# Half of one chunk's first product moved to Strassen's form, with its activations, sums and loads rearranged

## The chip, the core and the metric

The kernel runs on one core of a Trainium2 chip. A core has TensorE (PE: matmuls; its weight loads are listed apart as PEld), VectorE (DVE), ScalarE (ACT), GpSimd (POOL) and SyncE (SP, which here only issues transfers). Each engine works through its own queue in order, and semaphores make one wait for another. Matmul results go to PSUM, which has eight banks of 512 fp32 columns; everything else is in SBUF. The metric is the device time of one execution in microseconds (us), lower is better. Times below are from the start of the profiled span.

## The reference

Two stages. The first is a linear attention: q is put through a softmax over the head dimension, k through one over the sequence; per batch and head a 64 x 64 matrix kv is formed, and q times kv is the output. The second is a feed-forward layer with Silu between two products.

```python
q_s = softmax(q, axis=-1); k_s = softmax(k, axis=2)     # 8 batches, 8 heads, 576 rows, 64 columns
kv  = einsum('bhsd,bhse->bhde', k_s, v)
x   = einsum('bhsd,bhde->bhse', q_s, kv)                 # laid out as 4608 x 512
h   = x @ w_in                                           # 512 x 2048
out = (h * sigmoid(h)) @ w_out                           # 2048 x 512
```

Inputs and output are fp32.

## The kernel before, in words

The 4608 rows are taken in nine chunks of 512 columns of the transposed x (`XT`); batches have 576 rows, so chunk 0 is handled together with the 64 columns that follow it, and chunk 1 has only 448 columns of its own (`pieces(1)`, columns 64 to 511). For each chunk the first product (`XT` by `W1`, 16 blocks of 128 output features) and Silu give `GT0` or `GT1` in turn, and the second product (`GT` by `W2`) gives the output.

A list `units` holds closures that issue TensorE's work one after the other; `plan(u, f)` says which other operations are issued just before unit `u`. The last loop walks through the list. So the order on every engine is written out by hand: each engine's queue holds its operations in the order in which this walk meets them, and a late operation holds everything behind it on its engine.

Stages:

- Opening (to about 15 us): batch 0's loads on SP, W1's and W2's parts and batch 1's and 2's loads on GpSimd's queue; attention of batch 0.
- Wide phase, 16 units from about 15 to 33 us: chunk 0's first product with 576 columns (`wide_mm`, L256), two banks each, three pairs in turn. `silu` does Tanh on ScalarE (L248, h times half the sum of one and tanh(h/2) is Silu) and one combining operation on VectorE (L249). Batch 1's exps stand on ScalarE between the tanhs: `exp_q` (L108) before units 9 and 11, `exp_k` (L111) before 13 and 15. The sums of `q` go by `qsum_pair` on GpSimd (L124, L127), `qsum_end` on VectorE and `qnorm` (L155), on GpSimd for the first half and on VectorE for the second.
- From `b1` on (33 us), 32 units: chunk 0's second product, 16 plain blocks `mm2_plain` (L396) into banks 2 to 5, and chunk 1's first product, 16 plain blocks `mm1` (L276) of four matmuls with 448 columns, into banks 0 to 3; the first ten second-product blocks go alone, then the two kinds in turn, then the ten remaining first-product blocks alone. Between them: transposes (`tr`, L173) and `kv` (L187) and `xt` (L226) of batch 1, then those of batch 2, whose q is transposed by a DMA on SP (`q_transpose`, L165).
- `full(t)`, t from 2 to 6, 28 units each of eight matmuls with 256 columns, and two more chunks in the same form without new loads. Here both products are in Strassen's form as Winograd wrote it: seven products in the place of eight, for the price of sums. The first product of chunk t (`group`, L359, two halves g of eight blocks each) alternates with the second of chunk t-1 (`prod`, L458). The sums need `WS` (of W1, `ws_op` L312), `XS` (of XT, `xs_op` L321), `T` (of W2, `t_op` L442) and `S` (of GT, `s_op` L432). `group` puts products 1, 6, 7 and 4 into banks 0 and 1, and 2, 5 and 3 into banks 2 and 3; `group_snap` copies the first pair out to `h` (ScalarE, or VectorE where said), `group_add` adds the second pair to it on VectorE (L337), and `group_silu` is a Silu on ScalarE (L343) from `h` or straight from PSUM.
- `end`: the last chunk's second product. Products 1, 2, 6, 5, 7, 4, 3 in turn; `part` combines and stores the pieces (L705, L720).

Before the change the W sums are made here: `WS` and the first two `T` on VectorE between `b1`+3 and `b1`+20, and T4 and T3 (in place of a part of W2) on GpSimd at `b1`+22. The loads of batch 3 are issued on SP before unit `b1`+20, those of batch 2 on GpSimd before 10 (q), `b1` (k) and `b1`+6 (v).

`ld` has two buffers for each of `qt`, `kt`, `vt`, so a load waits until the half of the batch before it has been read. One `h0`, `h1`, `h2` each exist. `eq` has one buffer.

Of the kernel before, what the change touches and what calls it, by code (L numbers as in the profile page):

```python
# [12 lines left out]
ALU = mybir.AluOpType  # L13
# [4 lines left out]
def kernel(  # L18
# [86 lines left out]
    def exp_q(b, cc):  # L105
        if "eq" not in st[b]:
            st[b]["eq"] = ap.tile([128, J, NG * D], BF16, name="eq")
        nc.scalar.activation(out=half(st[b]["eq"], cc), in_=jgd(b, "qt", cc), func=ACT.Exp)  # L108
# [162 lines left out]
    A1_BANKS = [0, 1, 0, 1, 0, 1, 2, 0, 3, 1, 0, 2, 1, 0, 2, 3]  # L271

# [11 lines left out]
    def mm1_silu(t, fb, bank):  # L284
        o0 = pieces(t)[0][3]
        silu(t, fb, PS[:, bank, o0:TCH], GTS[t % 2][:, fb, o0:TCH], TCH - o0)

    def mm1(t, i):
        mm1_mm(t, FB[i], A1_BANKS[i], range(NC))
        mm1_silu(t, FB[i], A1_BANKS[i])  # L290

# [5 lines left out]

    def wa(c, f):
        return W1[:, 2 * c:2 * c + 2, f * 128:(f + 4) * 128]

    def xb(t, c, n):
        return XTS[t % 2][:, 2 * c:2 * c + 2, (1 - n) * HT:(2 - n) * HT]
# [11 lines left out]
    def xs_op(t, i):  # L314
        in0, in1 = {
            1: (xb(t, 0, 1), xb(t, 0, 0)),
            2: (xb(t, 1, 1), XS4[0]),
            3: (xb(t, 1, 1), xb(t, 0, 1)),
            4: (xb(t, 1, 0), XS4[1]),
        }[i]  # L320
        nc.vector.tensor_tensor(out=XS4[i - 1], in0=in0, in1=in1, op=ALU.subtract)  # L321

    def group_out(t, f, n):
        return GTS[t % 2][:, f:f + 4, (1 - n) * HT:(2 - n) * HT]

    def four(x):
        return x.rearrange("p (f n) -> p f n", f=4)

    def group_bank(bank):
        return PS[:, bank:bank + 2, :].rearrange("p b (f n) -> p (b f) n", f=2)  # L330

    def group_snap(i, eng=nc.scalar):
        H[i] = mp.tile([128, 2 * TCH], FP32, name=f"h{i}", bufs=1)
        copy(eng, H[i], PS[:, 0:2, :].rearrange("p b n -> p (b n)"))

    def group_add(i):
        nc.vector.tensor_tensor(  # L337
            out=H[i], in0=PS[:, 2:4, :].rearrange("p b n -> p (b n)"), in1=H[i], op=ALU.add
        )

    def group_silu(t, i, f, n):
        x = group_bank(0) if i is None else four(H[i])
        nc.scalar.activation(out=group_out(t, f, n), in_=x, func=ACT.Silu, scale=1.0 / XS)  # L343

    def group(t, g, i, on=None, defer=False):
        bank = 0 if i in (1, 6, 7, 4) else 2
# [10 lines left out]
        for p in range(4):  # L357
            for c in range(2):
                nc.tensor.matmul(  # L359
                    out=PS[:, bank + p // 2, (p % 2) * HT:(p % 2 + 1) * HT],  # L360
                    lhsT=a[:, c, p * 128:(p + 1) * 128],
                    rhs=bb[:, c, :],
# [5 lines left out]
        if i == 1:  # L368
            group_snap(0)
        elif i == 2:  # L370
            group_add(0)
        elif i == 6:
            group_snap(1, on.get(1, nc.scalar))
        elif i == 7:
            group_snap(2, on.get(2, nc.scalar))
            group_add(2)
        elif i == 4:
            group_silu(t, None, f1, 0)
        elif i == 3:
# [3 lines left out]
            group_add(1)  # L383
# [245 lines left out]
    a1 = [lambda i=i: mm1(1, i) for i in range(NFB)]  # L629

    units += [lambda i=i: mm2_plain(0, i) for i in range(10)]
    for i in range(10, NFB):
        units += [a1[i - 10], lambda i=i: mm2_plain(0, i)]
    units += a1[NFB - 10:]
    four_pairs = "ggbgbgbgbbgbgb"


# [65 lines left out]
    def part(name, bank, th, n, a):  # L703
# [13 lines left out]
            (0, 1): (nc.scalar, nc.gpsimd) if a == 0 else (nc.sync, nc.sync),  # L717
# [7 lines left out]
    def end(i, m):  # L725
        if i in (5, 3):
            prod(last, i, m, bank=(4, 0)[m], fresh=(i == 5), done=(i == 3))
        elif i == 4:
            prod(last, i, m, bank=1, fresh=(m == 0), done=(m == 1))
        else:  # L730
            prod(last, i, m, bank=5 if i == 2 else 3)
        if i == 3:
            part("sb", (4, 0)[m], 0, 1, m)
        elif m == 1 and i in (1, 6, 7):
            snap(last, {1: "sa", 6: "sb", 7: "sc"}[i], 3)
# [6 lines left out]
        elif m == 1 and i == 4:  # L742
            part("sc", 1, 1, 0, 0)
            part("sc", 1, 1, 0, 1)
# [8 lines left out]
    def loads(b, eng):  # L753
        for name, src in (("qt", q), ("kt", k), ("vt", v)):
            for cc in range(2):
                load(b, name, src, cc, eng)

    plan(9, lambda: (load_w2(8, 12), exp_q(1, 0), qsum_pair(1, 0)))
    plan(10, lambda: (load(2, "qt", q, 0, nc.gpsimd), load(2, "qt", q, 1, nc.gpsimd)))
# [76 lines left out]
```

## Time and profile before

| | |
|---|---|
| median of 4 runs | 266.0 us (265.73 to 266.6) |
| the profiled execution | 266.6 us, span 264.8 us |
| TensorE busy | 254.4 us (96%), 2708 matmuls |
| VectorE busy | 210.5 us (79%) |
| ScalarE busy | 182.7 us (69%) |
| GpSimd busy | 75.7 us (29%) |
| granted TensorE clock | 0.999 of full speed |
| from 35 to 55 us: TensorE, VectorE, ScalarE, GpSimd busy | 19.3, 19.4, 11.1, 10.7 of 20 |
| from 55 to 75 us | 19.7, 17.4, 15.3, 12.9 of 20 |
| T4, T3 on GpSimd | 4.07 and 4.06 us, at 57.2 and 61.3 |

Matmuls overlap, so a busy TensorE is not one at its peak: the distance from start to start says more. In the rows of the timeline the columns are: start, duration (of all merged instructions together), engine, source line, operation, output and inputs with shapes, count, and in brackets the idle time before it with what released it. In the chain of work that ended last each piece is start, duration, and what worked or was waited for.

### The profile page before, as it was taken

How to read it: one execution, taken by the hardware profiler on the slowest of the kernel's cores; microseconds unless marked ns; L12 is line 12 of the kernel's file. 1: busy time of each engine (PE TensorE's matmuls, PEld its weight loads, DVE VectorE, ACT ScalarE, POOL GpSimd, SP SyncE). 2: the span in 40 equal slices, each digit the busy share in tenths (PEclk: the TensorE clock that was granted, in tenths of full speed). 3: DMA queues.
4: the chain of work that ended last, by engine and by line, in shares of the span. 5: the costliest groups of instructions: out<-in, count | busy, mean ns of one | idle time of the engine just before them, and what ended most of it. 6: DMA issues, size and time to landing. Idle time of an engine off the chain costs nothing.

```text
span 264.8 us, 6375 instructions
## 1 busy us (share of the span) xinstructions
PE 254.4 (96%) x2708; PEld 200.8 (76%) x2708; DVE 210.5 (79%) x276; ACT 182.7 (69%) x209; POOL 75.7 (29%) x65
## 2 busy tenths in 40 slices
PE   8799999999999999999999999999999999999993
PEld 3357644445888888878888888888888888888782
DVE  2966789987997999789979997999798448855832
ACT  5756964749796699659966996699664757584610
POOL 1743991498341305030513050305000000000004
PEclk9999999999999999999999999999999999999999
DMA  7999999569987488747964887450416003300634
GB/s 253 333 189 339 253 332 334 214 121 378 333 308 138 163 188 305 160 143 149 336 137 164 186 305 154 153 125 0 92 22 139 0 2 81 80 2 1 131 69 119
DMA packets 35452, 45.89 MB, mean 173 GB/s; under 512 B 16208, under 2 KB 19984, under 8 KB 35424
## 3 DMA queue, kind: packets, MB, share of 16 engines
q1 hardware_dynamic: 29568, 33.69, 45.8%
q0 software_dynamic: 5616, 11.60, 16.7%
q8 instruction: 21, 0.34, 0.5%
q10 hardware_dynamic: 240, 0.20, 0.3%
q14 instruction: 7, 0.06, 0.1%
HBM read 36.70 MB, written 9.44 MB: 174 GB/s over the span
## 4 chain that ended last, share of the span: by engine, by line
PE 63%; DVE 17%; DMA 9%; issue 4%; POOL 3%; ACT 2%; POOLq 0%; DVEq 0%; ACTq 0%
PE PS L458 30%; PE PS L359 26%; DMA qt<-in_q_dram 5%; DVE GT L249 3%; DVE h L337 3%; DMA qT<-eq 2%; DVE zq L146 2%; DVE S L432 2%; PE PS L276 2%; PE PS L226 2%; PE PS L187 1%; DMA W<-in_moe_w_in_dram 1%; DVE WS L312 1%; PE PS L396 1%; DVE zq L148 1%
## 5 line engine op out<-in xcount | busy, mean ns | idle before, releaser
L337 DVE TENSOR_TENSOR h<-PS,h 128x1024 f32<-128x1024 f32 x42 | 50.7, 1206 | 11.6 <-PE PS L359 6.2
L458 PEld LDWEIGHTS <-GT 128*128 128x128 f16 x512 | 49.6, 98 | 7.4 <-issue 1.6
L458 PE MATMUL PS<-W,GT 128*128 128x256 f16 x384 | 49.1, 273 | 0.4 <-DVE h L337 0.4
L359 PEld LDWEIGHTS <-WS 128*128 128x128 f16 x448 | 43.7, 98 | 5.7 <-issue 0.7
L155 POOL TENSOR_TENSOR eq<-eq,rzq 128x1152 bf16<-128x1152 bf16 x13 | 27.5, 2117 | 59.2 <-DVE rzq L150 59.2
L359 PE MATMUL PS<-XS,WS 128*128 128x256 f16 x336 | 43.5, 273 | 0.1
L343 ACT ACTIVATE GT<-h 128x1024 f16<-128x1024 f32 x42 | 43.3, 1054 | 0.3 <-DVE h L337 0.3
L89 ACT COPY h<-PS 128x1024 f32<-128x1024 f32 x32 | 32.4, 1012 | 13.7 <-PE PS L359 13.3
L458 PEld LDWEIGHTS <-S 128*128 128x128 f16 x384 | 37.2, 98 | 5.2 <-issue 1.0
L359 PEld LDWEIGHTS <-W 128*128 128x128 f16 x336 | 32.5, 98 | 4.4 <-issue 0.2
L458 PE MATMUL PS<-T,S 128*128 128x256 f16 x256 | 32.7, 273 | 0.0
L249 DVE SCALAR_TENSOR_TENSOR GT<-sg,PS 128x576 f16<-128x576 f32 (+1 forms) x32 | 21.2, 679 | 9.1 <-ACT sg L248 8.9
L359 PE MATMUL PS<-XT,W 128*128 128x256 f16 x224 | 27.9, 273 | 0.0
L343 ACT ACTIVATE GT<-PS 128x1024 f16<-128x1024 f32 x14 | 14.3, 1023 | 19.4 <-PE PS L359 19.4
L248 ACT ACTIVATE sg<-PS 128x576 f32<-128x576 f32 (+1 forms) x32 | 18.8, 597 | 10.2 <-PE PS L276 5.4
L91 POOL CAST vaug<-vt 128x1152 bf16<-128x1152 f32 x12 | 15.0, 1256 | 35.6 <-DMA vt<-in_v_dram 34.8
L720 POOL DMA_DIRECT2D out_dram<-ow x5 | 2.7, 546 | 72.7 <-DVE ow L705 72.7
L108 ACT ACTIVATE eq<-qt 128x1152 bf16<-128x1152 f32 x16 | 18.6, 1165 | 2.7 <-DMA qt<-in_q_dram 2.5
L146 DVE TENSOR_REDUCE zq<-eq 128x18 f32<-128x1152 bf16 x12 | 16.1, 1344 | 3.9 <-ACT eq L108 3.9
L111 ACT ACTIVATE ek<-kt 128x1152 bf16<-128x1152 f32 x16 | 18.5, 1154 | 1.1 <-DMA kt<-in_k_dram 1.1
L256 PE MATMUL PS<-XT,W 128*128 128x288 f16 x128 | 16.7, 286 | 1.3 <-DVE GT L249 0.6
L256 PEld LDWEIGHTS <-W 128*128 128x128 f16 x128 | 12.3, 98 | 5.8 <-issue 1.9
(78 smaller groups left out, 354.4 us busy)
## 6 DMA issues: line engine op xcount, KB each, us to landing
out_dram<-ow SPq DMA_DIRECT2D x64, 128.0 KB, 2.4
qt<-in_q_dram SPq DMA_DIRECT2D x12, 576.0 KB, 4.8
kt<-in_k_dram SPq DMA_DIRECT2D x12, 576.0 KB, 6.1
vt<-in_v_dram SPq DMA_DIRECT2D x12, 576.0 KB, 5.6
qt<-in_q_dram POOLq DMA_DIRECT2D x4, 576.0 KB, 13.7
kt<-in_k_dram POOLq DMA_DIRECT2D x4, 576.0 KB, 13.9
vt<-in_v_dram POOLq DMA_DIRECT2D x4, 576.0 KB, 12.4
W<-in_moe_w_out_dram POOLq DMA_DIRECT2D x4, 512.0 KB, 15.1
```

Source lines behind the costliest of these rows:

```text
L89: eng.copy(out=o, in_=i)
L108: nc.scalar.activation(out=half(st[b]["eq"], cc), in_=jgd(b, "qt", cc), func=ACT.Exp)
L111: nc.scalar.activation(out=half(ek, cc), in_=jgd(b, "kt", cc), func=ACT.Exp)
L146: nc.vector.reduce_sum(out=z, in_=e, axis=AX.X)
L155: eng.tensor_tensor(out=e, in0=e, in1=r[:, :, :, None].to_broadcast([128, J, 2, D]), op=ALU.mult)
L248: nc.scalar.activation(out=s, in_=i, func=ACT.Tanh, scale=OS)
L249: nc.vector.scalar_tensor_tensor(out=o, in0=s, scalar=1.0, in1=i, op0=ALU.add, op1=ALU.mult)
L256: nc.tensor.matmul(out=PS[:, 2 * (fb % 3) + n, 0:S // 2], lhsT=W1[:, c, fb * 128:(fb + 1) * 128], rhs=XTS[0][:, c, n * (S // 2):(n + 1) * ...
L337: nc.vector.tensor_tensor(out=H[i], in0=PS[:, 2:4, :].rearrange("p b n -> p (b n)"), in1=H[i], op=ALU.add)
L343: nc.scalar.activation(out=group_out(t, f, n), in_=x, func=ACT.Silu, scale=1.0 / XS)
L359: nc.tensor.matmul(out=PS[:, bank + p // 2, (p % 2) * HT:(p % 2 + 1) * HT], lhsT=a[:, c, p * 128:(p + 1) * 128], rhs=bb[:, c, :], start=(i ...
L458: nc.tensor.matmul(out=PS[:, bank, m * HN:(m + 1) * HN], lhsT=a[:, fc, m * 128:(m + 1) * 128], rhs=bb[:, fc, :], start=(first and fc == 0) ...
```

## The change

Chunk 1's first product is split. Feature blocks 4 to 7 and 12 to 15 are made by `group(1, 1, ...)`, seven groups in Strassen's form over two halves of 224 columns, placed between chunk 0's last plain blocks in the pattern that `full` uses: nine plain blocks, then seven groups and seven plain blocks. The other eight blocks are plain as before, after them, in banks 0 to 3 in turn. Both halves get Silu on ScalarE instead of Tanh and a VectorE operation. The group helpers learn widths and bank pairs: for chunk 1 products 2, 5 and 3 use banks 6 and 7. There is one unit less (31 in the place of 32).

Around it: batch 1's `exp_q` are split into four halves in the wide phase and its `exp_k` moved to `b1`+1 and `b1`+2; the q2 loads are placed apart and the k2 loads moved to `b1`+3; the `XS` sums of chunk 1 are new; T1, T2, T4 and T3 are whole operations on VectorE from `b1`+22 to `b1`+30, as are WS1 to WS4 of half 0; the loads of batch 3 go to `b1`+24, v first, behind the first stores of chunk 0. In `end`, products 1, 6, 7 use bank 1 and product 4 bank 3, and one of the last stores goes to ScalarE's queue.

```diff
-    def exp_q(b, cc):
+    def exp_q(b, cc, g0=0, g1=2):
...
-        nc.scalar.activation(out=half(st[b]["eq"], cc), in_=jgd(b, "qt", cc), func=ACT.Exp)
+        nc.scalar.activation(
+            out=half(st[b]["eq"], cc)[:, :, g0:g1], in_=jgd(b, "qt", cc)[:, :, g0:g1], func=ACT.Exp
+        )
...
-    A1_BANKS = [0, 1, 0, 1, 0, 1, 2, 0, 3, 1, 0, 2, 1, 0, 2, 3]
...
-    def mm1(t, i):
-        mm1_mm(t, FB[i], A1_BANKS[i], range(NC))
-        mm1_silu(t, FB[i], A1_BANKS[i])
+    def mm1(t, fb, bank):
+        o0 = pieces(t)[0][3]
+        mm1_mm(t, fb, bank, range(NC))
+        nc.scalar.activation(
+            out=GTS[t % 2][:, fb, o0:TCH], in_=PS[:, bank, o0:TCH], func=ACT.Silu, scale=1.0 / XS
+        )
...
+    def span(t, n):
+        o0 = pieces(t)[0][3]
+        w = (TCH - o0) // 2
+        return slice(o0 + (1 - n) * w, o0 + (2 - n) * w)
+
+    def width(t):
+        return (TCH - pieces(t)[0][3]) // 2
...
     def xb(t, c, n):
-        return XTS[t % 2][:, 2 * c:2 * c + 2, (1 - n) * HT:(2 - n) * HT]
+        return XTS[t % 2][:, 2 * c:2 * c + 2, span(t, n)]
...
+    def group_bank(t, y):
+        bank = (6 if t == 1 else 2) if y else 0
+        return PS[:, bank:bank + 2, :].rearrange("p b (f n) -> p (b f) n", f=2)[:, :, 0:width(t)]
...
-    a1 = [lambda i=i: mm1(1, i) for i in range(NFB)]
-
-    units += [lambda i=i: mm2_plain(0, i) for i in range(10)]
-    for i in range(10, NFB):
-        units += [a1[i - 10], lambda i=i: mm2_plain(0, i)]
-    units += a1[NFB - 10:]
     four_pairs = "ggbgbgbgbbgbgb"
+    b0 = [lambda i=i: mm2_plain(0, i) for i in range(NFB)]
+    gs = [lambda i=i: group(1, 1, i, None, True) for i in ORDER]
+    units += [b0.pop(0) for _ in range(9)]
+    units += [{"b": b0, "g": gs}[x].pop(0) for x in four_pairs]
+    units += [lambda i=i: mm1(1, FB[i], i % 4) for i in range(HF)]
...
-            (0, 1): (nc.scalar, nc.gpsimd) if a == 0 else (nc.sync, nc.sync),
+            (0, 1): (nc.scalar, nc.gpsimd) if a == 0 else (nc.sync, nc.scalar),
...
-            prod(last, i, m, bank=1, fresh=(m == 0), done=(m == 1))
+            prod(last, i, m, bank=3, fresh=(m == 0), done=(m == 1))
         else:
-            prod(last, i, m, bank=5 if i == 2 else 3)
+            prod(last, i, m, bank=5 if i == 2 else 1)
...
-    plan(9, lambda: (load_w2(8, 12), exp_q(1, 0), qsum_pair(1, 0)))
-    plan(10, lambda: (load(2, "qt", q, 0, nc.gpsimd), load(2, "qt", q, 1, nc.gpsimd)))
-    plan(11, lambda: (exp_q(1, 1), qsum_end(1, 0), qnorm(1, 0, nc.gpsimd), qsum_pair(1, 1)))
-    plan(13, lambda: exp_k(1, 0))
-    plan(15, lambda: exp_k(1, 1))
+    plan(9, lambda: (load_w2(8, 12), exp_q(1, 0, 0, 1)))
+    plan(10, lambda: (exp_q(1, 0, 1, 2), qsum_pair(1, 0)))
+    plan(10, lambda: load(2, "qt", q, 0, nc.gpsimd))
+    plan(12, lambda: (exp_q(1, 1, 0, 1), qsum_end(1, 0), qnorm(1, 0, nc.gpsimd)))
+    plan(13, lambda: (exp_q(1, 1, 1, 2), qsum_pair(1, 1)))
+    plan(14, lambda: load(2, "qt", q, 1, nc.gpsimd))
+    plan(b1 + 1, lambda: exp_k(1, 0))
+    plan(b1 + 2, lambda: exp_k(1, 1))
...
-    plan(b1, lambda: (load(2, "kt", k, 0, nc.gpsimd), load(2, "kt", k, 1, nc.gpsimd)))
+    plan(b1 + 3, lambda: (load(2, "kt", k, 0, nc.gpsimd), load(2, "kt", k, 1, nc.gpsimd)))
...
-    plan(b1 + 9, lambda: (ws_op(3, 1), ws_op(4, 1)))
-    plan(b1 + 8, lambda: t_op(1, nc.vector, 0, 4))
-    plan(b1 + 9, lambda: t_op(1, nc.vector, 4, 8))
...
-    plan(b1 + 18, lambda: t_op(2, nc.vector, 0, 4))
-    plan(b1 + 20, lambda: t_op(2, nc.vector, 4, 8))
-    plan(b1 + 20, lambda: loads(3, nc.sync))
...
-    plan(b1 + 10, lambda: (ws_op(1, 0), ws_op(2, 0), ws_op(3, 0)))
-    plan(b1 + 11, lambda: ws_op(4, 0))
-    plan(b1 + 22, lambda: (t_op(4, nc.gpsimd), t_op(3, nc.gpsimd)))
+    plan(b1 + 8, lambda: (ws_op(3, 1), ws_op(4, 1)))
+    plan(b1 + 10, lambda: (xs_op(1, 1), xs_op(1, 2), xs_op(1, 3), xs_op(1, 4)))
...
+    plan(b1 + 17, lambda: exp_k(2, 1))
+    plan(b1 + 17, lambda: (vcast(2, 0, nc.gpsimd), vcast(2, 1, nc.gpsimd)))
+    plan(b1 + 22, lambda: (group_silu(1, 2, 4, 1), group_silu(1, 0, 12, 0)))
+    plan(b1 + 22, lambda: t_op(1, nc.vector))
+    plan(b1 + 23, lambda: mm2_plain_out(0, (0, 1)))
+    plan(b1 + 24, lambda: group_silu(1, 1, 12, 1))
+    plan(b1 + 24, lambda: (ws_op(1, 0), ws_op(2, 0)))
+    plan(b1 + 24, lambda: [load(3, x, y, i, nc.sync) for x, y, i in (
+        ("vt", v, 0), ("vt", v, 1), ("qt", q, 0), ("kt", k, 1), ("kt", k, 0), ("qt", q, 1)
+    )])
+    plan(b1 + 25, lambda: kv_both(2))
+    plan(b1 + 26, lambda: t_op(2, nc.vector))
+    plan(b1 + 27, lambda: xt(2, 0, nc.vector))
+    plan(b1 + 28, lambda: t_op(4, nc.vector))
+    plan(b1 + 29, lambda: xt(2, 1))
+    plan(b1 + 29, lambda: (ws_op(3, 0), ws_op(4, 0)))
     plan(b1 + 30, lambda: mm2_plain_out(0, (2, 3)))
+    plan(b1 + 30, lambda: t_op(3, nc.vector))
```

The other exps, sums and casts of batch 2 keep their kind and engines and move by a few units (`exp_q` to `b1`+10 and +13, `exp_k` to `b1`+14 and +17); XT's evacuation for the first half of chunk 2 moves from ScalarE to VectorE.

## The prediction

> **What bounds the kernel now.** The page's chain of work that ended last comes first: it says which engine the end hangs on.
>
> ```profile
> PE 63%; DVE 17%; DMA 9%; issue 4%; POOL 3%; ACT 2%; POOLq 0%; DVEq 0%; ACTq 0%
> ```
>
> TensorE holds 63%, but VectorE holds 17%, about 45 us, so I asked for the same chain in order of time between 15 and 95 us.
>
> ```profile
> 42.58 0.60 DVE T L442
> ...
> 51.85 0.49 DVE GT L249
> ...
> 66.98 0.35 DVE XS L321
> ...
> 82.12 1.23 DVE h L337
> 83.35 0.04 issue
> 83.39 1.03 PE PS L359 x8
> ```
>
> Most of the chain from 42.6 to 83.4 us is VectorE: chunk 1's first product and the first two thirds of `full(2)` follow VectorE's queue. After 83.39 it is TensorE, back to back at 0.874 us per unit of eight matmuls, up to the end. So what the change does to the middle is read on VectorE, at the first `xs_op` of `full(2)` (66.9 us): everything to 83.39 hangs on it. TensorE's timeline shows the units that are replaced, and one of Strassen's form:
>
> ```profile
> 45.23 0.92 PE L276 MATMUL PS<-XT,W 128*128 128x448 f16 x4
> 45.99 1.03 PE L396 MATMUL PS<-W,GT 128*128 128x512 f16 x4
> 46.85 0.92 PE L276 MATMUL PS<-XT,W 128*128 128x448 f16 x4
> ...
> 65.44 2.19 PE L359 MATMUL PS<-XT,W 128*128 128x256 f16 x16
> ```
>
> From start to start, a plain block of the first product takes 0.76 us and a block of the second 0.86. `full(2)` begins at 65.44. At the end, the chain and TensorE's timeline show a last stall:
>
> ```profile
> 246.56 1.04 PE L458 MATMUL PS<-W,S 128*128 128x256 f16 x8
> 246.76 1.22 DVE L337 TENSOR_TENSOR h<-PS,h 128x1024 f32<-128x1024 f32 x1 [0.53 <-PE PS L359]
> ...
> 248.04 3.65 PE L458 MATMUL PS<-W,GT 128*128 128x256 f16 x32 [0.44 <-DVE h L337]
> ```
>
> TensorE was free at 246.56 + 0.874 = 247.43 and started `end`'s first product at 248.04, when `group_add` had read bank 3.
>
> **Part by part.**
>
> *TensorE's work.* Eight blocks go from 8 x 4 matmuls of 448 columns (8 x 0.758 = 6.06 us) to 7 x 8 of 224. No row has 224 columns: 448 take 189.5 ns and 256 take 109.3, so 0.418 ns per column gives 95.9 ns, 0.77 us a group, 5.38 us in all. Bounds: in proportion to 256 columns, 5.35; no faster than 256, 6.12. I take 5.38: -0.7 us, but only where TensorE is the bound.
>
> *Wide phase.* Batch 1's exps (1.16 us each, before 26.1 to 33.9 us) become four half exps of about 0.67 (the vaug cast of 128x576 takes 0.67), and the two `exp_k` move behind the phase. TensorE's waits there (0.40 at 28.69, 0.20 at 31.00) should go. But the next thing on TensorE is `tr(1,0)`, which started at 33.15 because GpSimd's `qnorm` (30.96 + 2.13) ended at 33.09. In the new order the exp of both halves ends at about 27.9 instead of 27.3, the sums on GpSimd end at 30.2 instead of 29.55, and one load issue (0.72) instead of two (1.44) stands ahead of `qnorm`: it starts at about 30.95 again. Gain 0; TensorE waits at `tr` instead. What is late next is `tr(1,1)` (38.44, waited for VectorE's `qnorm`, 36.24 + 2.15; the same form took 1.36 at 7.32). VectorE now reaches it some 0.2 earlier, and one GpSimd load issue stands before the copy instead of the two k loads: between 0 and -0.45 (TensorE itself is ready at 38.0). I take -0.45, since the handed-over wait is shorter.
>
> *Loads.* In the trace GpSimd's loads land one after another, about 1.45 us apart, until the last v load of batch 2 (41.8 + 10.5 = 52.3). The queue stays full in the new order, so k of batch 2 still lands near 47.8 and 49.3, ahead of its exps at about 50 and 52. The second q2 load goes past GpSimd's `qnorm` and sums and still waits in that line. Cost 0; if k were over 1.5 us later, ScalarE's snapshot behind it would hold `group(7)`'s bank.
>
> *Tanh to Silu.* 16 tanh of 0.54 on ScalarE and 16 combining operations of 0.54 (8.6 us) on VectorE go. Instead: three snapshots, four group Silus of about 0.93 (1.02 less 128 columns), eight Silus of about 0.56. Silu needs another table: two more loads.
>
> ```profile
> 75.00 1.28 ACT L343 ACT_TABLE_LOAD   x1
> ```
>
> The row says 1.28 us each, with operations directly before and after. The Trainium skill ("ScalarE: Activation LUTs", What ACT_TABLE_LOAD costs) puts a switch at about 2.66 us with its drain[...]. With 1.28, the first load ends before `group(4)` is done and the Silu frees bank 0 some 0.7 us before the first `mm1`; with 2.66 that `mm1` would wait 0.7. The second stands at the head of `full(2)`, where ScalarE waited 0.60 and 0.97 for TensorE. I take the row: 0 on the path.
>
> *VectorE's order is what decides.* With `g1` at about 43.9, the units to the last group are 7 x 0.77 + 6 x 0.865 + 0.28 (group 2 waits for the second `xt` evacuation) = 10.9 us: group 3 ends at 54.8. VectorE has little to do before it, then everything is queued behind `group_add(1)`: 1.0 for it, T1 1.15, one eviction 0.60, WS1 and WS2 1.33, `kvcopy` 0.70, T2 1.15, the XT evacuation 1.13, T4 1.15, WS3 and WS4 1.2, an eviction 0.6, T3 1.15 (128x2048 f16 takes 1.22 alone, 1.15 from start to start; the others from their own rows), together 11.2 us. From 55.0 the first `xs_op` is at 66.15 against 66.90. TensorE needs only 0.85 + 8 x 0.758 + 0.84 (kv) + 0.68 (two xt) = 8.4 us for the same stretch and is at `full(2)` by about 64, so it will wait for XS2 in group 6.
>
> To this comes GpSimd. Moving T3 and T4 off it leaves it only casts, but SP's q, k and v loads of batch 3 move behind the first four stores, from 57.1 to about 59.7, v now first. v lands near 63.9 and 65.3 (4 us and a bit after issue; 3.7 to 4.7 for the first of a row in the trace), so both casts fall into T4, WS3, WS4, T3. How such pairs go:
>
> ```profile
> 49.94 4.19 POOL L155 TENSOR_TENSOR eq<-eq,rzq 128x1152 bf16<-128x1152 bf16 x2 [7.45 <-DVE rzq L150]
> 52.77 1.91 DVE L442 TENSOR_TENSOR T<-W,T 128x1024 f16<-128x1024 f16 x1
> 54.08 3.17 POOL L91 CAST vaug<-vt 128x1152 bf16<-128x1152 f32 x2
> 55.13 1.10 DVE L442 TENSOR_TENSOR T<-W,T 128x1024 f16<-128x1024 f16 x1
> ```
>
> The same VectorE operation takes 0.68 alone. It started at 52.77 and ended 0.6 after GpSimd's operation: it stood still meanwhile. The Trainium skill ("SBUF — State Buffer", Who interferes with whom) says that a VectorE instruction with two SBUF inputs and a GpSimd one that reads SBUF exclude each other. By the rule two casts of 1.16 cost up to 2.3; by a share of the port, half of it. But two of the operations there are evictions from PSUM, which are free beside GpSimd (0.61 at 54.60). Bounds 0 to 2.1; I take 1.0. In exchange the casts leave `full(2)`, where the S sum took 1.49 instead of 1.21: -0.3. Sum for the middle: 66.15 + 1.0 - 0.3 - 66.90 = -0.05 us. VectorE's saved 8.6 us end as idle time before 55 us.
>
> SP: qT of batch 2 is issued near 53.5, lands 4.7 later and is wanted at 60. q of batch 3 lands near 66.8; ScalarE can exp it from 67.3 (snapshot, then table load). Cover 0.5, and the k exps behind it have 2 us until the snapshot of group 7 waits for them.
>
> *The end.* `end`'s products 1, 6, 7 use bank 1, which ScalarE's Silu reads by 244.82 + 1.02 = 245.84. Product 1 then starts at 247.43: -0.6. Behind it, product 2 at 249.18 needs the Silu that ended at 249.08: it just fits. The last store goes to ScalarE's queue, free at 261.23, instead of behind SP's first (261.4): 0.
>
> Sum: -0.05 - 0.6 = -0.65 us. The profiled execution took 266.6 (span 264.8 and 1.8 around it), so 265.95 of it; the median of the runs is 266.0, which gives **265.4 us**.
>
> **Rivals.** (1) TensorE sets the middle: casts fall on PSUM operations, VectorE reaches XS2 by 66. Then the middle gains the 0.75 of 66.15 against 66.90 and the 0.3, up to 1.3 if TensorE never waits: 264.2 to 264.9. For it: VectorE is idle from 44 to 55; against: 11.2 us of queue against 8.4 of TensorE. (2) The end's gain is all there is to pay for the locks: casts cost 1.6, the middle +0.55, total about 0: 265.8 to 266.2. For it: the three T sums stand exactly where v lands. (3) Slower: VectorE's queue behind `group_add(1)` is longer than summed: 11.2 us without any reserve, after it the chain has no idle until 84.47. From the first `xs_op` at 67.8 on (0.9 later than now, 0.3 of it given back, 0.6 paid by the end) it is a loss; with locks of 2.1 and 0.8 more for the sums (128x2048 in place takes 1.92 on the mean of all its rows) it is at 69.05 and the time 267.2. (4) The bank swap does nothing, since product 1 waits for another Silu: 266.0; its first Silu ended at 246.75, so unlikely, and I count it with (2).
>
> **How the numbers follow.** Forecast 0.40 (its own range 264.9 to 265.9), rival 1 0.20, rivals 2 and 4 0.20, rival 3 0.20. A measurement of this kernel can tell about 0.2%, 0.53 us, so faster means below 265.5. Faster: 0.35 of the forecast's 0.40 and rival 1, 0.55. Same: the rest of it and most of rivals 2 and 4, 0.21. Slower: 0.24. The range leaves out the outer half of rivals 1 and 3: 264.2 to 266.9.
>
> **What would show it.** Right: `tr(1,0)` still at 33.1; groups of 224 at 0.77; VectorE without a gap from 55 to the end of the `xs_op`s near 68; TensorE waiting for XS in group 6 of `full(2)`; two casts of batch 3 beside lengthened T or WS sums; no wait of `end`'s first product. Wrong: `full(2)` on TensorE from its first unit (rival 1), a first `xs_op` after 67.8 (rival 3), exps of batch 3 that wait for their loads, or a stall between group 1 and group 3.

## The result

| | before | after |
|---|---|---|
| median | 266.0 us (62 runs, 264.84 to 267.09) | 265.01 us (41 runs, 264.61 to 266.14) |
| ratio to before, 95% interval | | 0.9967 [0.9959, 0.9975] |
| profiled execution, span | 266.6 us, 264.8 us | 265.05 us, 263.3 us |

The change makes the kernel 0.9 us faster (0.7 to 1.1). The forecast was 265.4 us with 264.2 to 266.9 around it. The two profiled executions differ by 1.55 us, more than the medians do, mostly because loads landed later in the profiled execution of before (TensorE waited 0.45 us for a part of W1 at 24.69); so the stages below are measured from one landmark to the next, not from zero.

First the page's chain of work that ended last, by engine, for the kernel after:

```profile
PE 77%; DVE 11%; DMA 4%; POOL 2%; ACT 2%; issue 2%; SPq 1%; POOLq 0%; DVEq 0%; ACTq 0%
```

VectorE went from 17% of the chain to 11%, and TensorE from 63% to 77%; a part of that is the opening, where the chain of before ran for 13.68 us through a load of q (DMA, 9% there and 4% here). The chain in order of time (start, duration, what) shows the middle:

```profile
32.62 0.68 PE PS L175 x9
...
53.43 0.78 PE PS L368 x8
...
54.23 0.04 DVE h L346
54.27 0.97 issue
55.24 1.22 DVE T L451
```

From 32.6 to 54.2 us the end now hangs on TensorE (but for one XT evacuation on ScalarE, 0.91 at 43.30); in before VectorE had most of it from 42.6 on, and took turns with TensorE and ScalarE between 52.4 and 64. The hand-over to VectorE comes at the `group_add` behind the last Strassen group. TensorE's timeline of the kernel after shows the new groups, the start of `full(2)` and its wait:

```profile
43.18 2.00 PE L368 MATMUL PS<-XT,W 128*128 128x224 f16 x16
45.02 1.03 PE L405 MATMUL PS<-W,GT 128*128 128x512 f16 x4
45.88 0.93 PE L368 MATMUL PS<-XS,WS 128*128 128x224 f16 x8
46.65 1.03 PE L405 MATMUL PS<-W,GT 128*128 128x512 f16 x4
...
63.18 1.91 PE L368 MATMUL PS<-XT,W 128*128 128x256 f16 x16
64.93 1.04 PE L467 MATMUL PS<-W,GT 128*128 128x256 f16 x8
67.65 1.05 PE L368 MATMUL PS<-XS,WS 128*128 128x256 f16 x8 [1.68 <-DVE XS L329]
```

A group takes 46.65 - 45.88 = 0.77 us. TensorE reaches `full(2)` 30.56 us behind `tr(1,0)` (63.18 - 32.62), 1.7 us sooner than in before (65.44 - 33.15 = 32.29), and then waits 1.68 ahead of the group that needs XS2. What VectorE did meanwhile, in its timeline:

```profile
54.23 1.09 DVE L346 TENSOR_TENSOR h<-PS,h 128x896 f32<-128x896 f32 x1 [2.10 <-PE PS L368]
55.24 1.22 DVE L451 TENSOR_TENSOR T<-W 128x2048 f16<-128x2048 f16 x1
...
64.11 1.65 DVE L451 TENSOR_TENSOR W<-W 128x2048 f16<-128x2048 f16 x1
65.69 1.37 DVE L329 TENSOR_TENSOR XS<-XT 128x512 f16<-128x512 f16 x1
67.16 0.43 DVE L329 TENSOR_TENSOR XS<-XT,XS 128x512 f16<-128x512 f16 x1
```

and GpSimd's casts of batch 3 beside it:

```profile
63.54 1.16 POOL L91 CAST vaug<-vt 128x1152 bf16<-128x1152 f32 x1 [8.52 <-DMA vt<-in_v_dram]
65.08 1.71 POOL L91 CAST vaug<-vt 128x1152 bf16<-128x1152 f32 x1 [0.38 <-DMA vt<-in_v_dram]
```

VectorE has no gap from 54.23 on. T3 takes 1.65 instead of 1.22 and the first `xs_op` 1.37 instead of 0.42. The ends fit strict turns, to within 0.2 us: T3 stands from 64.11 until the first cast ends at 64.70; the second cast, begun at 65.08, stands until T3 ends at 65.76; the `xs_op` stands until that cast ends at 66.79. ScalarE's timeline:

```profile
64.31 1.01 ACT L89 COPY h<-PS 128x1024 f32<-128x1024 f32 x1 [0.15 <-PE PS L368]
67.79 1.28 ACT L108 ACT_TABLE_LOAD   x1 [2.46 <-DMA kt<-in_k_dram]
69.08 1.16 ACT L108 ACTIVATE eq<-qt 128x1152 bf16<-128x1152 f32 x1
```

It is idle 2.46 us for batch 3's loads. The end, on TensorE:

```profile
245.60 1.04 PE L467 MATMUL PS<-W,S 128*128 128x256 f16 x8
246.48 3.66 PE L467 MATMUL PS<-W,GT 128*128 128x256 f16 x32
```

The wait of 0.44 ahead of `end`'s first product is gone.

The time by stage, from start to start in TensorE's timelines (the landmarks are `tr(1,0)`, the pair of `group`s that merges into one row of 16 matmuls in `full(3)` and again in `full(4)`, and `end`'s first product), for all kernels that follow:

| kernel | `tr(1,0)` at | to `full(3)` | to `full(4)` | to `end` |
|---|---|---|---|---|
| before | 33.15 | 58.99 | 26.69 | 129.21 |
| end_alone | 32.42 | 59.39 | 26.61 | 128.61 |
| after | 32.62 | 59.06 | 26.19 | 128.61 |
| end_undone | 32.41 | 58.98 | 26.19 | 129.22 |
| exps_whole | 32.01 | 59.28 | 26.19 | 128.61 |
| plain_tanh_half | 32.20 | 60.17 | 26.51 | 128.61 |
| casts_on_scalar | 32.24 | 58.58 | 26.19 | 128.61 |
| sums_early | 32.32 | 58.80 | 26.19 | 128.62 |
| loads_early | 32.35 | 58.43 | 26.19 | 128.61 |
| sums_and_loads_early | 32.51 | 57.71 | 26.19 | 128.61 |
| sums_and_all_loads_early | 32.63 | 58.15 | 26.19 | 128.62 |
| casts_first | 32.43 | 59.36 | 26.19 | 128.61 |

What follows `end`'s first product takes 16.8 us in every one. After and `end_undone`, whose middle is the same, agree to 0.1 us in the second column. Before and `end_alone` differ by 0.4 there because `tr(1,0)` lies differently behind the opening. Counted from the wide phase's first matmul, `full(3)` begins at 76.30 in `end_alone`, 76.81 in before (with the 0.45 for W1), 76.12 in after and 76.04 in `end_undone`.

### The profile page after: what moved, and what is told of

Same layout as the page of the kernel before. It is cut to its first block, busy times and chain, and to the rows that moved or that the text cites. A ratio compares the mean times of both kernels' runs of the same rounds, so it can differ in the third digit from the quotient of the medians.

```text
span 263.3 us, 6409 instructions
## 1 busy us (share of the span) xinstructions
PE 252.6 (96%) x2732; PEld 203.4 (77%) x2732; DVE 208.3 (79%) x268; ACT 186.6 (71%) x211; POOL 66.7 (25%) x63
## 3 DMA queue, kind: packets, MB, share of 16 engines
q0 software_dynamic: 5616, 11.60, 16.8%
## 4 chain that ended last, share of the span: by engine, by line
PE 77%; DVE 11%; DMA 4%; POOL 2%; ACT 2%; issue 2%; SPq 1%; POOLq 0%; DVEq 0%; ACTq 0%
PE PS L467 33%; PE PS L368 31%; PE PS L405 5%; DMA vt<-in_v_dram 4%; PE PS L258 3%; PE PS L228 2%; DVE h L346 2%; PE PS L189 2%; DVE T L451 1%; DVE zq L148 1%; DVE WS L319 1%; SPq L97 1%; DVE S L441 1%; DVE GT L441 1%; DVE XS L329 1%
## 5 line engine op out<-in xcount | busy, mean ns | idle before, releaser
L346 DVE TENSOR_TENSOR h<-PS,h 128x1024 f32<-128x1024 f32 (+1 forms) x45 | 53.9, 1199 | 13.8 <-PE PS L368 7.8
L368 PEld LDWEIGHTS <-WS 128*128 128x128 f16 x480 | 46.7, 98 | 8.7 <-DVE XS L329 2.0
L368 PE MATMUL PS<-XS,WS 128*128 128x256 f16 (+1 forms) x360 | 46.3, 272 | 1.8 <-DVE XS L329 1.7
L352 ACT ACTIVATE GT<-h 128x1024 f16<-128x1024 f32 (+1 forms) x45 | 46.1, 1047 | 0.3 <-DVE h L346 0.3
L89 ACT COPY h<-PS 128x1024 f32<-128x1024 f32 (+1 forms) x35 | 35.1, 1003 | 13.1 <-PE PS L368 12.6
L368 PE MATMUL PS<-XT,W 128*128 128x256 f16 (+1 forms) x240 | 29.5, 272 | 0.1
L352 ACT ACTIVATE GT<-PS 128x1024 f16<-128x1024 f32 (+1 forms) x15 | 15.2, 1016 | 18.9 <-PE PS L368 18.9
L108 ACT ACTIVATE eq<-qt 128x1152 bf16<-128x1152 f32 (+1 forms) x18 | 19.0, 1058 | 2.5 <-DMA qt<-in_q_dram 2.4
L467 PE MATMUL PS<-W,S 128*128 128x256 f16 x128 | 16.5, 273 | 0.0
L487 DVE SCALAR_TENSOR_TENSOR ow<-PS,sc 128x512 f32<-128x512 f32 x7 | 4.8, 691 | 14.4 <-ACT sc L483 14.4
```

The costliest lines, as they stand in the source:

```text
L89: eng.copy(out=o, in_=i)
L108: nc.scalar.activation(out=half(st[b]["eq"], cc)[:, :, g0:g1], in_=jgd(b, "qt", cc)[:, :, g0:g1], func=ACT.Exp)
L346: nc.vector.tensor_tensor(out=four(t, i), in0=group_bank(t, True), in1=four(t, i), op=ALU.add)
L368: nc.tensor.matmul(out=PS[:, bank + p // 2, (p % 2) * HT:(p % 2) * HT + width(t)], lhsT=a[:, c, p * 128:(p + 1) * 128], rhs=bb[:, c, 0:wid ...
L467: nc.tensor.matmul(out=PS[:, bank, m * HN:(m + 1) * HN], lhsT=a[:, fc, m * 128:(m + 1) * 128], rhs=bb[:, fc, :], start=(first and fc == 0) ...
```

## The experiments

Each ratio is to the kernel before, run beside it on the same chip, with its 95% interval.

**The end's part alone, and all but it.** `end_alone` is the kernel before with only the end's edits:

```diff
-            (0, 1): (nc.scalar, nc.gpsimd) if a == 0 else (nc.sync, nc.sync),
+            (0, 1): (nc.scalar, nc.gpsimd) if a == 0 else (nc.sync, nc.scalar),
...
-            prod(last, i, m, bank=1, fresh=(m == 0), done=(m == 1))
+            prod(last, i, m, bank=3, fresh=(m == 0), done=(m == 1))
...
-            prod(last, i, m, bank=5 if i == 2 else 3)
+            prod(last, i, m, bank=5 if i == 2 else 1)
...
-            snap(last, {1: "sa", 6: "sb", 7: "sc"}[i], 3)
+            snap(last, {1: "sa", 6: "sb", 7: "sc"}[i], 1)
...
-            part("sc", 1, 1, 0, 0)
-            part("sc", 1, 1, 0, 1)
+            part("sc", 3, 1, 0, 0)
+            part("sc", 3, 1, 0, 1)
```

> The kernel before with the change's end alone: products 1, 6, 7 of the last second product in bank 1, product 4 in bank 3, the last store split over two queues. Theory (the end pays about 0.6 us by the bank, the rest of the gain comes from the middle): 265.4 against 266.0, ratio 0.998, and no wait of TensorE between the last unit of the last chunk and the end's first product (0.6 us in the kernel before). Rival (the whole gain of 1.0 us is the end): ratio 0.996. Rival (the bank swap moves the stall to product 2): ratio 1.000.

`end_undone` is the kernel after with the same lines taken back.

> The changed kernel with the end put back to banks 3 and 1 and one queue. Theory: the middle's gain alone remains, 0.4 to 0.5 us, 265.5 to 265.6, ratio 0.998, and the wait ahead of the end's first product is back at about 0.6 us. Rival (the whole gain is the end): ratio 1.000.

`end_alone`: 265.34 us, 0.9982 [0.9961, 1.0002], an interval that just reaches no change. `end_undone`: 265.40 us, 0.9988 [0.9977, 0.9999]. TensorE in `end_alone`:

```profile
246.16 1.04 PE L458 MATMUL PS<-W,S 128*128 128x256 f16 x8
247.03 3.66 PE L458 MATMUL PS<-W,GT 128*128 128x256 f16 x32
```

and in `end_undone`:

```profile
245.32 1.04 PE L467 MATMUL PS<-W,S 128*128 128x256 f16 x8
246.80 3.65 PE L467 MATMUL PS<-W,GT 128*128 128x256 f16 x32 [0.44 <-DVE h L346]
```

The wait goes and comes with the banks, in both surroundings, and the last column of the table says 0.60 us each time. What is left for everything else in the change is 0.12% of 266, 0.3 us (0.0 to 0.6), by the medians.

**Batch 1's exps as before.** `exps_whole` is the kernel after with the wide phase's exps, sums and q2 loads as they were:

```diff
-    plan(9, lambda: (load_w2(8, 12), exp_q(1, 0, 0, 1)))
-    plan(10, lambda: (exp_q(1, 0, 1, 2), qsum_pair(1, 0)))
...
-    plan(12, lambda: (exp_q(1, 1, 0, 1), qsum_end(1, 0), qnorm(1, 0, nc.gpsimd)))
...
-    plan(b1 + 1, lambda: exp_k(1, 0))
-    plan(b1 + 2, lambda: exp_k(1, 1))
+    plan(9, lambda: (load_w2(8, 12), exp_q(1, 0), qsum_pair(1, 0)))
...
+    plan(11, lambda: (exp_q(1, 1), qsum_end(1, 0), qnorm(1, 0, nc.gpsimd), qsum_pair(1, 1)))
+    plan(13, lambda: exp_k(1, 0))
+    plan(15, lambda: exp_k(1, 1))
```

> The changed kernel with batch 1's exps as before the change: whole q exps before units 9 and 11, k exps in the wide phase, both q2 loads together. Theory (the transposition after the wide phase waits for GpSimd's qnorm in either form; only the next one, held by VectorE's qnorm, gains): first transposition at the same distance from the wide phase's start, the second 0.4 us later than in the changed kernel; 265.4, ratio to the kernel before 0.998. Rival (the spread exps save the 0.75 us of waits in the wide phase): 265.8, ratio 0.9995. Rival (they are worth nothing, because VectorE sets the later stage): 265.0, ratio 0.9967.

264.99 us, 0.9968 [0.9953, 0.9983]: the same as after. Its two transpositions on TensorE:

```profile
32.01 0.68 PE L175 MATMUL PS<-ident,eq 128*128 128x128 bf16 x9
...
37.13 0.68 PE L175 MATMUL PS<-ident,eq 128*128 128x128 bf16 x9
```

With whole exps they are 5.12 us apart, with spread ones 4.83 (32.62 and 37.45 in after); but the first comes at 32.01 instead of 32.2 to 32.6. That is the opening's doing: counted from the wide phase's first matmul, the first transposition starts 16.91 us behind with whole exps (in `exps_whole` and in `end_alone`) and 17.06 with spread ones, so the spreading costs 0.15 there. The second is 22.03 behind in `exps_whole` and 21.89 in after. The spreading gains 0.14 in all by these traces, and by the medians nothing that can be measured.

**Strassen's form against plain blocks.** `plain_tanh_half` is the kernel after with eight plain blocks in the place of the seven groups, by the same Tanh and VectorE operation as in before (ScalarE's switch to Silu then comes at 55.93 instead of 52.09); all W2 sums, loads and the end stay as after.

```diff
-    gs = [lambda i=i: group(1, 1, i, None, True) for i in ORDER]
+    def mm1_tanh(t, fb, bank):
+        o0 = pieces(t)[0][3]
+        mm1_mm(t, fb, bank, range(NC))
+        silu(t, fb, PS[:, bank, o0:TCH], GTS[t % 2][:, fb, o0:TCH], TCH - o0)
+
+    late = [lambda i=i: mm1_tanh(1, FB[HF + i], (0, 1, 6, 7)[i % 4]) for i in range(HF)]
+    gs = late[0:6] + [lambda: (late[6](), late[7]())]
...
-    plan(b1 + 10, lambda: (xs_op(1, 1), xs_op(1, 2), xs_op(1, 3), xs_op(1, 4)))
...
-    plan(b1 + 22, lambda: (group_silu(1, 2, 4, 1), group_silu(1, 0, 12, 0)))
...
-    plan(b1 + 24, lambda: group_silu(1, 1, 12, 1))
```

> The changed kernel with the seven Strassen groups replaced by eight plain blocks with Tanh and the VectorE operation, in the same units; all else stays. Theory: TensorE needs 0.68 us more there and VectorE's last operation of chunk 1 comes about 0.6 us later than its group_add did, so the queue behind it too: 0.3 to 0.6 us slower than the changed kernel, 265.4 to 265.6, ratio to the kernel before 0.9985. Rival (the saving on TensorE is worth nothing, because VectorE sets the end of the stage): as the changed kernel, 265.0, ratio 0.9967.

266.42 us, 1.0024 [1.0006, 1.0042], so 0.57% or 1.5 us above after, where at most 0.6 had been expected. By the table 1.1 of it is lost before `full(3)` and 0.32 behind it. On TensorE:

```profile
43.83 1.30 PE L276 MATMUL PS<-XT,W 128*128 128x448 f16 x6 [0.52 <-ACT XT L89]
```

on VectorE:

```profile
56.00 1.22 DVE L451 TENSOR_TENSOR T<-W 128x2048 f16<-128x2048 f16 x1
```

A plain block needs both evacuations of XT (0.52 us of waiting): the first two blocks lose 0.7 us to them (42.76 to 44.96, where two take 1.52), the first two groups only 0.3 (43.18 to 45.02, where two take 1.54). And eight blocks take 0.7 us more than seven groups. T1 starts 23.8 us after `tr(1,0)`, against 22.6 in after. So the time that Strassen's form saves on TensorE counts, although VectorE sets the end behind it: the queue of sums starts only when TensorE has done the last group. That plain blocks with Silu would do the same was not run. The 0.32 is a different matter (last section).

This run shows one more thing. It has plain blocks and the new end, as `end_alone` has, and differs from it by the new places of the sums (T4 and T3 on VectorE instead of GpSimd), loads and exps, and by Silu in its other half. Yet it is 1.1 us slower by the ratios (1.0024 against 0.9982, 0.4 to 1.8 us), and `full(3)` begins 0.9 later behind the wide phase's first matmul (77.23 against 76.30). So the new arrangement costs about as much as the groups bring in it, and the middle as a whole hardly moved. Which of the moves costs how much was not taken apart, but for the sums and loads below.

**The casts beside the sums.** `casts_on_scalar` is the kernel after with batch 3's two v casts on ScalarE, one unit after the start of `full(2)`:

```diff
-            plan(u + (2, 11)[i], lambda i=i: vcast(b, i, nc.gpsimd))
+            if t == 2:
+                plan(u + 1, lambda i=i: vcast(b, i, nc.scalar))
+            else:
+                plan(u + (2, 11)[i], lambda i=i: vcast(b, i, nc.gpsimd))
```

> The changed kernel with the two v casts of batch 3 on ScalarE behind the first snapshot of full(2), where it waits for q, so that GpSimd reads nothing from SBUF while VectorE makes T3 and XS. Theory (GpSimd's casts hold VectorE): T3 falls from 1.65 to 1.22 and the first xs_op from 1.37 to 0.42, group 6 on TensorE starts about 1.3 us earlier than 67.65. In time little of it is left, because ScalarE's exps of batch 3 (q at 67.8) then hold group 4: 264.8, ratio to the kernel before 0.9955. Rival (VectorE was held by something else, for instance the XT evacuation): T3 and the first xs_op stay at 1.65 and 1.37.

264.31 us, 0.9935 [0.9916, 0.9954]. VectorE:

```profile
63.74 1.22 DVE L451 TENSOR_TENSOR W<-W 128x2048 f16<-128x2048 f16 x1
64.87 0.42 DVE L329 TENSOR_TENSOR XS<-XT 128x512 f16<-128x512 f16 x1
```

TensorE:

```profile
65.88 1.05 PE L368 MATMUL PS<-XS,WS 128*128 128x256 f16 x8 [0.29 <-DVE XS L329]
...
73.36 1.03 PE L368 MATMUL PS<-XS,W 128*128 128x256 f16 x8 [1.04 <-ACT h L89]
```

Without a cast on GpSimd both operations are back at their own lengths, and the wait for XS2 falls from 1.68 to 0.29: the 1.4 us were the casts'. Only part of it reaches the end, since the casts (now 2.22 us on ScalarE) and then the late exps hold ScalarE's snapshot, for which TensorE waits 1.04. By the table 0.48 us come out, by the medians 0.7, more than expected.

**W2's sums spread.** `sums_early` is the kernel after with T1 and two WS sums where VectorE has little to do:

```diff
-    plan(b1 + 8, lambda: (ws_op(3, 1), ws_op(4, 1)))
+    plan(b1 + 8, lambda: (ws_op(3, 1), ws_op(4, 1), t_op(1, nc.vector)))
+    plan(b1 + 18, lambda: (ws_op(1, 0), ws_op(2, 0)))
...
-    plan(b1 + 22, lambda: t_op(1, nc.vector))
...
-    plan(b1 + 24, lambda: (ws_op(1, 0), ws_op(2, 0)))
```

> The changed kernel with T1 and the sums WS1 and WS2 of half 0 moved ahead of the last group_add, into time in which VectorE idles (b1+8 and b1+18). Theory A (VectorE's queue behind that group_add is all that holds group 6 of the next chunk): first xs_op 2.4 us earlier than 65.7, TensorE's wait of 1.7 us ahead of group 6 gone, time 263.7 to 264.0, ratio to the kernel before 0.992. Theory B (ScalarE is next: its exps of batch 3 wait for their q until 67.8 and hold the snapshot of group 7): TensorE waits less at group 6 and as much more ahead of group 4, gain 0.2 only, 264.8, ratio 0.9955.

264.76 us, 0.9959 [0.9946, 0.9971]. VectorE's queue behind the last `group_add` is 2.4 us shorter by these sums, but 0.26 us comes out by the table. VectorE:

```profile
57.18 0.18 DVE L200 RECIPROCAL rz<-PS 128x4 f32<-128x4 f32 x1 [0.95 <-PE PS L189]
...
64.23 1.37 DVE L329 TENSOR_TENSOR XS<-XT 128x512 f16<-128x512 f16 x1
65.70 1.19 DVE L329 TENSOR_TENSOR XS<-XT,XS 128x512 f16<-128x512 f16 x1
```

TensorE:

```profile
66.95 1.05 PE L368 MATMUL PS<-XS,WS 128*128 128x256 f16 x8 [1.78 <-DVE XS L329]
```

ScalarE:

```profile
67.67 1.28 ACT L108 ACT_TABLE_LOAD   x1 [3.15 <-DMA qt<-in_q_dram]
```

The first `xs_op` comes only 1.2 us earlier behind `tr(1,0)` (64.23 - 32.32 = 31.91, against 33.07), since VectorE now waits 0.95 for `kv`. And v is not earlier: both casts (63.48 to 66.63) now stand beside the `xs_op`s, which take 1.37 and 1.19 instead of 0.42 each, so TensorE waits 1.78 for XS2, no less than in after. q of batch 3 does not come sooner either. The number is that of theory B, but by luck: B had the wait move from group 6 to group 4, and TensorE waits only 0.27 there.

**The loads ahead of the stores.** `loads_early` leaves the sums as in after and issues batch 3's q and k before the first stores, v where it was:

```diff
-    plan(b1 + 24, lambda: [load(3, x, y, i, nc.sync) for x, y, i in (
-        ("vt", v, 0), ("vt", v, 1), ("qt", q, 0), ("kt", k, 1), ("kt", k, 0), ("qt", q, 1)
+    plan(b1 + 18, lambda: [load(3, x, y, i, nc.sync) for x, y, i in (
+        ("qt", q, 0), ("kt", k, 1), ("kt", k, 0), ("qt", q, 1)
     )])
+    plan(b1 + 24, lambda: [load(3, "vt", v, i, nc.sync) for i in range(2)])
```

> The changed kernel with the q and k loads of batch 3 directly behind the transposition, the v loads behind the stores as before; the sums stay late. Theory: v lands some 3 us later (69), so the casts leave T3 and the first xs_op (1.3 us), and ScalarE's exps no longer hold the snapshot: group 6 about 1.3 us earlier, in time 0.8 to 1.0 less than the changed kernel, 264.1, ratio 0.993. Rival (VectorE's queue alone decides, the early sums made the gain of the run before): within 0.3 of the changed kernel, ratio 0.996.

`sums_and_loads_early` is `sums_early` with this edit.

> As the run with the early sums, and the q and k loads of batch 3 issued directly behind the transposition of batch 2 (b1+18), ahead of the stores; the v loads stay. Theory B: with q there by about 61 ScalarE's exps start some 2.5 us earlier, and both waits go: 263.7 to 264.0, ratio 0.992. Theory A: the loads add nothing, the same time as with the early sums alone. Rival: the loads share the DMA engines with the transposition, xt of chunk 2 waits up to 1 us: no gain against the changed kernel, 265.0.

`loads_early`: 264.14 us, 0.9938 [0.9915, 0.9960]. TensorE and GpSimd:

```profile
65.98 1.05 PE L368 MATMUL PS<-XS,WS 128*128 128x256 f16 x8 [0.29 <-DVE XS L329]
...
72.14 1.05 PE L467 MATMUL PS<-T,S 128*128 128x256 f16 x8 [0.70 <-DVE S L441]
```

```profile
68.98 4.13 POOL L91 CAST vaug<-vt 128x1152 bf16<-128x1152 f32 x2 [14.22 <-DMA vt<-in_v_dram]
```

As expected, v comes at 69 and the casts leave T3 (1.22) and the `xs_op` (0.42); they meet an S sum instead (1.99), for which TensorE waits 0.70. `sums_and_loads_early`: 263.65 us (262.92 to 264.78), 0.9920 [0.9900, 0.9941], which beats both kernels: 2.1 us below before. TensorE of `sums_and_loads_early`:

```profile
65.42 1.05 PE L368 MATMUL PS<-XS,WS 128*128 128x256 f16 x8
...
71.58 1.05 PE L467 MATMUL PS<-T,S 128*128 128x256 f16 x8 [0.70 <-DVE S L441]
```

its VectorE:

```profile
69.54 1.98 DVE L441 TENSOR_TENSOR S<-S,GT 128x2048 f16<-128x2048 f16 x1
```

and its GpSimd:

```profile
69.03 3.52 POOL L91 CAST vaug<-vt 128x1152 bf16<-128x1152 f32 x2 [13.19 <-DMA vt<-in_v_dram]
```

v comes at 69 here too, past the `xs_op`s. The wait for XS2 is gone, and ScalarE begins the table load ahead of the exps at 64.73 without a wait. The cast still finds a sum to stop: the second S sum takes 1.98 instead of 1.23, and TensorE waits 0.70 for it. By the table the two edits bring 0.26 and 0.63 alone and 1.35 together. The waits say why: the early sums alone leave XS2 to the casts, the early loads alone leave it to VectorE's queue (0.29). The medians (0.2 and 0.8 alone, 1.25 together, each to 0.3 to 0.6) cannot tell this from a plain sum.

**Two other places for that cast.** `sums_and_all_loads_early` issues all six loads at `b1`+18, v behind q and k:

```diff
     plan(b1 + 18, lambda: [load(3, x, y, i, nc.sync) for x, y, i in (
-        ("qt", q, 0), ("kt", k, 1), ("kt", k, 0), ("qt", q, 1)
+        ("qt", q, 0), ("kt", k, 1), ("kt", k, 0), ("qt", q, 1), ("vt", v, 0), ("vt", v, 1)
     )])
-    plan(b1 + 24, lambda: [load(3, "vt", v, i, nc.sync) for i in range(2)])
```

> Early sums and all six loads of batch 3 behind the transposition, v last. Theory: v lands near 66 and 67.5, so the casts fall on VectorE's group_add and snapshot, which read PSUM, and the wait of 0.7 us for the S sum (1.98 us beside a cast) of the run with v behind the stores goes: 263.1 to 263.3, ratio 0.990. Rival (the casts are only moved onto other sums): as that run, 263.65, ratio 0.992.

264.10 us, 0.9923 [0.9904, 0.9943]: no better, against an expectation of more. VectorE:

```profile
68.34 1.66 DVE L441 TENSOR_TENSOR S<-GT 128x2048 f16<-128x2048 f16 x1
70.10 1.99 DVE L441 TENSOR_TENSOR S<-S,GT 128x2048 f16<-128x2048 f16 x1
```

v came at 67.8 and 69.3, 1.3 us sooner, and met both S sums instead of one; TensorE waits 1.15.

`casts_first` has v first at `b1`+18, so that the casts end before the sums, and T2 early as well:

```diff
-    plan(b1 + 18, lambda: (ws_op(1, 0), ws_op(2, 0)))
+    plan(b1 + 18, lambda: (ws_op(1, 0), ws_op(2, 0), t_op(2, nc.vector)))
...
-        ("qt", q, 0), ("kt", k, 1), ("kt", k, 0), ("qt", q, 1), ("vt", v, 0), ("vt", v, 1)
+        ("vt", v, 0), ("vt", v, 1), ("qt", q, 0), ("kt", k, 1), ("kt", k, 0), ("qt", q, 1)
...
-    plan(b1 + 26, lambda: t_op(2, nc.vector))
```

> Early sums, T2 early too, and all six loads of batch 3 directly behind the transposition with v first, so that GpSimd's casts of batch 3 come near 60 to 63 us. Theory: they lengthen T4 and a WS sum by about 1 us each at most, which is paid by the reserve that the early T2 gives (1.15 us), and S1 and S2 of full(2) run at 1.22; no wait above 0.3 us from group 6 on: 263.0, ratio 0.989. Rival (q comes 3 us later and the exps hold the snapshot again, or the casts cost more than the reserve): 263.7 to 264.2, ratio 0.992.

265.17 us, 0.9970 [0.9952, 0.9989]: two us over the expectation, and over its rival's 264.2. VectorE:

```profile
53.22 1.52 DVE L319 TENSOR_TENSOR WS<-WS,W 128x1024 f16<-128x1024 f16 x1
54.66 2.17 DVE L451 TENSOR_TENSOR T<-W,T 128x2048 f16<-128x2048 f16 x1
```

GpSimd:

```profile
52.58 3.18 POOL L91 CAST vaug<-vt 128x1152 bf16<-128x1152 f32 x2
```

TensorE:

```profile
57.88 0.81 PE L189 MATMUL PS<-vaug,ek 64*64 64x65 bf16 x72 [1.50 <-DVE h L346]
```

The sums that were moved ahead of the last group met the casts of batch 2, which in after lie from 52.77 to 55.02, beside VectorE's wait for TensorE and a `group_add`, which reads one of its inputs from PSUM. A WS sum took 1.52 instead of 0.68 and T2 2.17 instead of 1.22; they held `group_add`, and TensorE waited 1.50 us for it. The WS sum took 1.52 in the other kernels with early sums too, and there `group_add` began only 0.6 later than in after (22.23 us behind `tr(1,0)` in `sums_early`, 21.61 in after); what was too much is T2 behind it. The casts of batch 3 did end before the `xs_op`s and S sums, as expected (60.18 and 61.67).

## Why the prediction was right, and where it was not

**The sum** was -0.05 for the middle and -0.6 for the end. The end is -0.60 in the table, and what follows its first product did not change, as said of the store's queue. The middle, counted from the wide phase's first matmul, is 0.2 us shorter than in `end_alone` (76.12 and 76.04 against 76.30): small, as said, and a little better than -0.05. The third difference, from `full(3)` to `full(4)`, is 26.19 against 26.69 and 26.61, about -0.46, and was in no step of the sum. Together these make 1.2 to 1.3 us where the medians show 0.9 (0.7 to 1.1), so the third difference may not be whole in every execution. That the measured 265.0 lies below the forecast of 265.4 comes mostly from this gain, which was not foreseen.

**VectorE's order decides, 11.2 us of queue.** Right. From `group_add` (54.23) to the first `xs_op` (65.69) are 11.46 us, 0.43 of it T3's wait for a cast: 11.03 without. VectorE had no gap, TensorE waited for XS in the group named. Counted from `tr(1,0)`, the queue began at 54.23 - 32.62 = 21.61 where 55.0 - 33.15 = 21.85 had been worked out. That these 0.24 and the 0.17 of the shorter queue paid for the next point is luck.

**Locks of 1.0** (the time for which GpSimd's casts hold VectorE's sums). The term was too small: 0.43 on T3 and 0.95 on the `xs_op`, 1.4 us, and `casts_on_scalar` shows both gone. The row of before with a lengthened T sum was the right one to reason from. The prediction weighed the rule of the Trainium skill ("SBUF — State Buffer", Who interferes with whom), that a VectorE instruction with two SBUF inputs and a GpSimd one reading SBUF exclude each other, at up to 2.3, against a share of the port at half of that. The turns worked out above (each waits for the end of the other's running instruction) agree with exclusion. The casts cost less than 2.3 mostly because the first had run for 0.6 of its 1.16 us beside the PSUM eviction at 63.51 before T3 came; the second cost 0.95. What the casts were to give back in `full(2)` was right: the first S sum took 1.21 instead of 1.49.

**Loads of batch 3.** v was expected at 63.9 and 65.3 and came at 63.54 and 65.08. q was expected at 66.8 with a cover of 0.5; ScalarE's first exp could start only at 67.79, after 2.46 us of waiting, so q was a microsecond late and there was no cover: ScalarE had been ready for the table load since 65.32. The first q load was issued at 60.26 and took 7.5 us to land, behind the two v loads, where the first v load took 4.3. Exps that wait for their loads were one of the prediction's own signs of being wrong; in after they cost nothing, because XS2 was still later. `sums_early` shows a first price: a wait of 0.27 for `h` at 73.67.

**TensorE's work.** Groups at 0.77 us: exact. But "-0.7 us, but only where TensorE is the bound", with VectorE taken as the bound, undervalued it, although the sum did let the queue begin when the groups end. Up to the last group TensorE is the bound, as the chain of after shows, and everything behind moves with it. `plain_tanh_half` puts Strassen's half, with the part of the wait for XT that it avoids, at 1.1 us in that stretch. The saved 8.6 us of VectorE's work did end as idle time, as said (2.10 us ahead of `group_add` alone).

**Silu.** The two further table loads took 1.28 us each with the next operation 0.01 to 0.02 us behind (67.79 + 1.28, then 69.08), so the row was right to prefer to the 2.66 of the Trainium skill ("ScalarE: Activation LUTs", What ACT_TABLE_LOAD costs). By the prediction's working the first `mm1` would have waited 0.7 us at 2.66; it started at 54.90, 0.87 behind the unit before it (54.03), without a wait.

**Wide phase 0, `tr(1,1)` -0.45.** The wait was handed over to `tr(1,0)`, as said: TensorE waits 0.52 there for GpSimd's `qnorm`, and one of the two waits in the wide phase stayed (0.19 at 30.96). The distance between the transpositions fell by 0.41 to 0.46 (5.29 and 5.24 to 4.83), so the second wait went as said too. But the first transposition lost 0.15, and `exps_whole`, which keeps the longer distance in part (5.12), is as fast.

**The rivals.** (1), TensorE setting the middle, was wrong in after, and is nearly what `sums_and_loads_early` comes to: TensorE without a wait for XS, and the time that (1) gave as its lower end, 264.2, is passed. (Its own terms, 0.6 for the end and 1.05 to 1.3 for the middle, make 264.1 to 264.4, not up to 264.9.) (2) was right in its mechanism, locks above 1.0, and wrong in their being decisive. (3) needed the first `xs_op` after 67.8; it came at 65.69 and ended at 67.06. (4) is refuted by the traces of both end kernels.

## What to carry to other kernels

Where an engine with slack works through a queue that opens with a wait for the bottleneck, look not at its busy time but at what stands behind that wait: sums that need nothing from the bottleneck belong ahead of it, and what delays the last producer delays the whole queue. Before such sums are moved, look which GpSimd operations on SBUF lie at the new place; casts of 1.16 us that were free beside an eviction or an idle VectorE held a sum for 0.8 to 0.95 us (`casts_first`, `sums_early`). And what is gained by moving the sums depends on where the loads then land, so the two are to be looked at together: by the traces 0.26 and 0.63 us apart, 1.35 together here. Strassen's groups show the same from the other side: what they bring has to be weighed against the sums and loads that had to move for them.

## What was not expected of the hardware

The DMA transposition of q that feeds `full(3)` is issued at the same place, among the same operations, in all kernels here. In before TensorE waits for it:

```profile
112.89 0.30 PE L226 MATMUL PS<-qT,kvn 64*64 64x256 bf16 x4 [0.29 <-DMA qT<-eq]
```

and in after it does not:

```profile
111.82 0.41 PE L228 MATMUL PS<-qT,kvn 64*64 64x256 bf16 x8
```

From issue to landing it took 6.2 us in before, 6.2 in `end_alone` and 6.1 in `plain_tanh_half`, and 4.6 to 5.1 in the nine other kernels. TensorE wants it 5.7 us after the issue in all of them, and the wait at this place is the whole 0.3 to 0.5 us of the third column. The slow ones are the three kernels without Strassen's groups in chunk 1. TensorE's and VectorE's operations around the transposition lie at the same distances in all; the one difference found is that SP's own instruction took 2.73 to 2.75 us in the three and 2.93 to 3.49 in the nine. That alone makes no slow landing: at 80.53 in before it took 2.75 and landed after 4.6. The later transpositions of one kernel scatter too, from 4.6 to 5.6 us in after. So it is open why chunk 1 should reach 50 us further, and whether every execution shows it; no run here settles it.

Also new was how a collision goes on. In the collisions here the operation that waits runs next, so two casts of 1.16 us and two sums stop each other in turn, and the casts grow too (1.71 in after; 4.13 for the pair in `loads_early`, where the pair of batch 2 took 2.26 beside an idle VectorE and a `group_add`).
